# Spare matmuls at TensorE's waits, and new issue slots for every block, in an attention-plus-snake kernel

## The chip, the cores and the metric

The kernel runs on one core of one Trainium2 chip. The metric is the device time of one execution in microseconds (us), as a median over runs; less is better. A profile is one more execution, recorded on the chip. Its span is about 1.8 us shorter than the time that is reported for the same execution, so spans are compared with spans and times with times. Each run also carries a mean granted TensorE clock (1.00 is full speed). A run is called slow if it is over 1.5% above the fastest of the same kernel; ratios use the other runs, called fast.

## The reference, cut to what matters

```python
# x (8, 8, 512, 64), state (8, 8, 32, 64)
scores = scale * x @ state^T ;  a  = softmax(scores)  ; xread = a @ state
scores2 = scale * state @ x^T ; a2 = softmax(scores2) ; sread = a2 @ x
y = concat(xread, sread)                    # (8 * 544, 512), heads side by side
h = y @ w_in                                # 512 -> 2048
g = h + sin(alpha * h)**2 / (alpha + 1e-9)  # "snake"
out = g @ w_out                             # 2048 -> 512
```

## The kernel before: the parts that matter

One block is one batch. In a block, sixteen slots f each compute one 128x512 tile h_ps (the attention weights AT times M, where M is state times w_in, made in four steps), its sine on ACT, the square of the sine on POOL or VectorE, and then "snake" on VectorE, which writes gT and frees the buffer of h_ps. There are four such buffers. The second product with w_out (`mm2`, tile o_ps) lags by a block and fills the gaps of TensorE. A ninth block does the rows of sread.

```python
psH = ...tile_pool(name="psH", bufs=4, PSUM)      # h_ps
psO = ...tile_pool(name="psO", bufs=2, PSUM)      # o_ps, and the spare matmuls
def warm_up(n):                                   # spare matmuls: zeros, nobody reads them
    if n: wp = psO.tile([P, S], FP32, ...)
    for _ in range(n): nc.tensor.matmul(wp[:], warm[:, 0:P], warm[:], ...)
def pack(a, g):                                   # L240: x of a batch, reordered, on VectorE
    nc.vector.tensor_copy(a.xp[...], xnat_l[a.b][...])
def mm1(t, f):
    ... matmuls h_ps ...
    nc.scalar.activation(s, hp, ACT.Sin, scale=alpha_sb[:, f])
    if f in SQ[kind(t)]: late.append((s2, s, n))  # square later, on VectorE (L410)
    else: nc.gpsimd.tensor_tensor(s2, s, s, mult) # square now, on POOL (L403)
def snake(...): nc.vector.scalar_tensor_tensor(gT, s2, inva, hp, mult, add)   # L413
...
for b in range(B):                                # which slot issues what; BATCH is a table
    p = BATCH[min(b, 3)]; s0 = (b - 1) * 16
    if b > 1: add(post, s0 + p["L"], load_x, b, 1)            # x of batch b, POOL writes descriptors
    if b: pack at s0 + p["P"]; scores at p["S"]; exp at p["X"]; row sums at p["R"]
          normalise at p["N"] (on POOL, or on VectorE for g in ND); AT at p["A"]
    m_step(b, k, p["MA"][k]) at b * 16 + p["M"][k]            # MA: copy on ACT (1) or VectorE (0)
for t in range(B + 1):
    for f in range(16):
        cur = mm1(t, f); <pe of this slot>; snake of two slots ago
        squares left from the slot before; <mm2 of this slot>; <post of this slot>
```

(Shortened; the whole kernel follows.)

The softmax here doesn't subtract the row's maximum and nothing guards it: scores larger than these inputs give would overflow.

Of the kernel before, what the change touches and what calls it, by code (L numbers as in the profile page):

```python
# [19 lines left out]



BATCH = {0: {'M': (-13, 0, 6, 7), 'MA': ((1, 0), (1, 1), (1, 0), (1, 1))},
 1: {'P': (1, 1),
     'T': (3, 3),
     'S': (3, 3),
     'X': (3, 3),
     'R': (4, 6),
     'N': (7, 10),
     'A': 13,  # L30
     'M': (-5, -2, 3, 9),
     'MA': ((1, 1), (1, 1), (1, 1), (0, 1)),
     'W': (5, 5)},
 2: {'L': -9,
     'P': (-1, -1),
     'T': 1,
     'S': (6, 6),
     'X': (6, 6),
     'R': (7, 9),
     'N': (7, 11),  # L40
     'A': 14,
     'M': (-5, -2, 6, 10),
     'MA': ((1, 1), (0, 0), (1, 1), (0, 1)),
     'W': (-1, -1)},
 3: {'L': -19,
     'P': (-12, -9),
     'T': -9,
     'S': (2, 2),
     'X': (2, 2),
     'R': (4, 5),  # L50
     'N': (4, 11),
     'A': 11,
     'M': (-3, 1, 4, 8),
     'MA': ((1, 1), (1, 1), (1, 1), (1, 1)),
     'W': (-1, -1)}}

SQ = {0: (0, 4, 8, 9, 12, 15),
 1: (3, 5, 6, 7, 11),
 2: (2, 5, 7, 8, 9, 12, 15),
 7: (0, 5, 6, 11, 13, 15),  # L60
 8: (0, 1, 2, 3, 6, 9, 13, 15)}
ND = {1: (), 2: (), 3: (0, 1)}
XS0 = 0

TWO0 = (0, 0, 0, 1, 3, 0, 3, 0, 0, 1, 2, 3, 2, 2, 2, 2)
TWO1 = (2, 5, 3, 1, 1, 3, 3, 0, 3, 4, 9, 3, 0, 1, 4, 1)
TWO = (3, 7, 3, 9, 2, 4, 9, 4, 2, 3, 1, 6, 3, 3, 2, 3)
WARM = (9, 2, 1, 1)
LATER = 6

LOADS = ('i0', 'i1', 'x1', 'o0', 'i2', 'i3', 'o1', 'o2', 'o3')
# [3 lines left out]
def kernel(  # L75
# [11 lines left out]
    B, H, S, D = x.shape  # L87
    Ns = state.shape[2]
    P = nc.NUM_PARTITIONS
# [97 lines left out]
    def warm_up(n):  # L187
        if n:
            wp = psO.tile([P, S], FP32, name="o_ps", tag="o")
        for _ in range(n):  # L190
            nc.tensor.matmul(wp[:], warm[:, 0:P], warm[:], start=True, stop=True)

    def kind(t):
        return t if t < 2 or t >= B - 1 else 2


    def prep_state():
        st2 = const.tile([P, 16, 2, D], BF16, name="st2")
        for half, copy in ((0, nc.vector.tensor_copy), (1, nc.scalar.copy)):
            js = slice(half * 8, (half + 1) * 8)  # L200
            copy(st2[:, js], st_nat[:, js].unsqueeze(2).to_broadcast([P, 8, 2, D]))
        for half in range(2):
            tp = psH.tile([P, 8, P], BF16, name="st_ps", tag="h")
            for k in range(8):
                nc.tensor.transpose(
                    tp[:, k, :],
                    st2[:, half * 8 + k].rearrange("p r d -> p (r d)"),
                    ident[:],
                )
            for r in range(2):  # L210
                rows = slice(r * D, (r + 1) * D)
                src = tp[rows].rearrange("d k (e r2 jh) -> d e r2 jh k", r2=2, jh=2)
                dst = stT[rows].rearrange(
                    "d bg (h2 r2 jh hf k) -> d (bg h2) r2 jh hf k", h2=2, r2=2, jh=2, hf=2
                )
                nc.scalar.copy(dst[:, :, r, :, half, :], src[:, :, r])

    def prep_alpha():
        tp = psH.tile([P, FT], FP32, name="al_ps", tag="h")
        nc.tensor.transpose(tp[:], alpha_rows[:], ident_f[:])  # L220
        nc.scalar.copy(alpha_sb[:], tp[:])
# [132 lines left out]
    def m_step(b, fs, on_act):  # L354
        if fs == 0:
            Ms[b] = mpool.tile([P, G, DFF], BF16, name="M")
        if b == 0 and fs == 0:
            mp = [psH.tile([P, FW], FP32, name="m0_ps", tag="h") for _ in range(G)]
        else:
            mp = [psX.tile([P, FW], FP32, name="m_ps", tag="px") for _ in range(G)]  # L360
        for h in range(2):
            for g in range(G):
                for r in range(2):
                    rows = slice(r * D, (r + 1) * D)
                    c0 = h * 2 * Ns + r * Ns
                    o0 = h * 2 * Ns + (r ^ g) * Ns
                    nc.tensor.matmul(  # L367
                        mp[g][o0:o0 + Ns, :],
                        stT[rows, b * G + g, c0:c0 + Ns],
                        w_in_sb[rows, 2 * g + h, fs * FW:(fs + 1) * FW],  # L370
                        start=True, stop=True,
                    )
        for g in range(G):
            dst = Ms[b][:, g, fs * FW:(fs + 1) * FW]
            if on_act[g]:
                nc.scalar.copy(dst, mp[g][:])  # L376
            else:
                nc.vector.tensor_copy(dst, mp[g][:])


    def mm1(t, f):
# [17 lines left out]
        s2 = sinp.tile([P, S], BF16, name="s2")  # L399
        if f in SQ[kind(t)]:  # L400
            late.append((s2, s, n))
# [58 lines left out]

    warm_up(WARM[0])
    prep_state()
    prep_alpha()
    warm_up(WARM[1])
    a = atts[0] = Att(0)
# [4 lines left out]
    a.T(1)  # L470
    warm_up(WARM[2])
    a.S(0)
# [6 lines left out]
        load(*w)  # L479
    a.Rs(1)  # L480
    a.N(1, nc.vector)
    m_step(0, 0, (True, True))
    a.W(psO, "o")
    a.Cs()
    warm_up(WARM[3])
    nc.scalar.activation(tiny[:, 1:2], warm[:, 0:1], ACT.Sin)
    a.AT_([0])
    a.AT_([1])
# [5 lines left out]
    pe, post, two = {}, {}, {}  # L494

    def add(d, s, fn, *args):
        d.setdefault(s, []).append((fn, args))
# [8 lines left out]
    for b in range(B):  # L506
        p = BATCH[min(b, 3)]
        s0 = (b - 1) * FT
        if b > 1:
            add(post, s0 + p["L"], load_x, b, 1)  # L510
        if b:
            add(post, s0 + p["P"][0], first, b)
            for g in range(G):
                add(post, s0 + p["P"][g], att, b, "pack", g)
            if b == 1:
                for g in range(G):
                    add(pe, s0 + p["T"][g], att, b, "T", g)
            else:
                add(post, s0 + p["T"], att, b, "T_dma")
            for g in range(G):  # L520
                add(pe, s0 + p["S"][g], att, b, "S", g)
                add(post, s0 + p["X"][g], att, b, "X", g)
                add(post, s0 + p["R"][g], att, b, "Rs", g)
                eng = nc.vector if g in ND[min(b, 3)] else nc.gpsimd
                add(post, s0 + p["N"][g], att, b, "N", g, eng)
            if b == 1:
                add(pe, s0 + p["A"], att, b, "AT_", [0, 1])
            else:
                add(post, s0 + p["A"], att, b, "AT_dma")
        s0 = b * FT  # L530
        if b:
            add(pe, s0 + p["W"][0], att, b, "W")
            add(pe, s0 + p["W"][1], att, b, "Cs")
        add(post, s0 + (p["W"][1] if b else XS0), att, b, "xs")
        for k in range(0 if b else 1, FS):
            add(pe, s0 + p["M"][k], m_step, b, k, p["MA"][k])

    def rows(t, counts, todo):
        for f, c in enumerate(counts):
            two[t * FT + f] = [args for args in todo[:c]]  # L540
            del todo[:c]

    todo = [(0, st, ft, ft + 1) for ft in range(FT) for st in (0, 1)]
    rows(0, TWO0, todo)
    todo += [(0, st, ft, ft + 1) for st in (2, 3) for ft in range(FT)]
    rows(1, TWO1, todo)
    assert not todo
    for t in range(2, B + 1):
        todo = [(t - 1, st, ft, ft + 1) for st in range(C) for ft in range(FT)]
        rows(t, TWO if t < B - 1 else (4,) * FT, todo)  # L550

# [53 lines left out]
```

## Time and profile before

| | before |
|---|---|
| median of 3 runs | 231.87 us (231.43 to 232.74) |
| span of the profile | 231.4 us |
| TensorE, VectorE, ACT, POOL busy | 94%, 75%, 73%, 46% |
| start of sin of f = 9, block 0 | 30.29 |
| start of sin of f = 12, block 0 | 33.34 |
| start of blocks 1, 2 and 8 (first sin) | 37.80, 58.99, 200.05 |

The last rows are milestones, read from ACT's records: the same instruction in two kernels shows how far one is ahead.

```profile
29.68 1.05 POOL L298 TENSOR_TENSOR A<-E,rR 128x512 bf16<-128x512 bf16 x1
30.67 0.95 POOL L143 DMA_DIRECT2D xnat<-in_x_dram  x1
31.73 1.03 POOL L403 TENSOR_TENSOR s<-s 128x512 bf16<-128x512 bf16 x1
```

Both squares took 0.75 us together, and there is a gap of 0.1 us between POOL's descriptors and its next square.

### The profile page before, as it was taken

The numbers are of one execution on the slowest core, as the hardware profiler recorded it, in microseconds if no ns is written. First come the engines' busy times: TensorE is split into PE (matmuls) and PEld (weight loads), VectorE is DVE, ScalarE is ACT, GpSimd is POOL, SyncE is SP. The second block draws the span as 40 slices with busy tenths as digits, with TensorE's granted clock in tenths as the row PEclk, the third lists the DMA queues.
The fourth block names the chain that finished last, engine by engine and source line by source line (L and its number), as shares of the span: only waits on it lengthen the run. The fifth ranks groups of instructions, "written<-read, shape, count | busy, mean of one in ns | idle before, by whom it ended". The sixth has DMA issues, their size and how long they took to land.

```text
span 231.4 us, 4164 instructions
## 1 busy us (share of the span) xinstructions
PE 216.4 (94%) x1508; PEld 103.7 (45%) x1534; DVE 174.4 (75%) x306; ACT 169.8 (73%) x277; POOL 106.4 (46%) x112
## 2 busy tenths in 40 slices
PE   7776989899999999999999999999999999999992
PEld 2534243444544444445444444444444444556562
DVE  3779589989969995998699878988698665744310
ACT  4696797898697769886988788878887876544420
POOL 3864398439732652366145705451543635123300
PEclk9996799999999999999999999999999999999999
DMA  6999998855915390449036702610212111111112
GB/s 218 189 202 206 206 125 112 203 74 111 132 52 136 91 139 18 133 123 139 1 113 162 113 23 93 165 62 4 87 49 78 57 49 47 48 45 47 48 47 92
DMA packets 36662, 23.36 MB, mean 101 GB/s; under 512 B 19728, under 2 KB 32288, under 8 KB 36640
## 3 DMA queue, kind: packets, MB, share of 16 engines
q0 software_dynamic: 11504, 7.87, 24.4%
q1 hardware_dynamic: 24864, 14.95, 21.8%
q10 hardware_dynamic: 272, 0.27, 0.4%
q8 instruction: 12, 0.20, 0.4%
q14 instruction: 10, 0.08, 0.1%
HBM read 17.31 MB, written 8.91 MB: 113 GB/s over the span
## 4 chain that ended last, share of the span: by engine, by line
PE 84%; DMA 6%; DVE 6%; issue 1%; POOL 1%
PE o_ps L422 48%; PE h_ps L386 22%; DMA xnat<-in_x_dram 4%; PE m_ps L367 4%; PE h_ps L392 3%; DVE gT L413 2%; PE s_ps L277 2%; DMA st_nat<-in_state_dram 2%; PE o_ps L447 2%; PE w_ps L322 1%; DVE xp L240 1%; PE w_ps L333 1%; POOL w_in_sb L166 1%; DVE s L410 0%; DVE rC L342 0%
## 5 line engine op out<-in xcount | busy, mean ns | idle before, releaser
L422 PE MATMUL o_ps<-w_out_sb,gT 128*128 128x512 bf16 x506 | 133.5, 381 | 2.5 <-issue 1.7
L403 POOL TENSOR_TENSOR s<-s 128x512 bf16<-128x512 bf16 (+1 forms) x84 | 87.2, 1045 | 104.6 <-ACT s L398 102.4
L398 ACT ACTIVATE s<-h_ps,alpha_sb 128x512 bf16<-128x512 f32 (+1 forms) x144 | 94.7, 672 | 37.4 <-PE h_ps L386 24.6
L413 DVE SCALAR_TENSOR_TENSOR gT<-s,inva_sb,h_ps 128x512 bf16<-128x512 bf16 (+1 forms) x144 | 99.6, 710 | 25.0 <-POOL s L403 23.3
L386 PE MATMUL h_ps<-AT,M 128*128 128x512 bf16 x252 | 76.0, 385 | 1.5 <-DVE gT L413 1.0
L422 PEld LDWEIGHTS <-gT 128*128 128x128 bf16 x528 | 48.7, 98 | 57.5 <-issue 7.6
L386 PEld LDWEIGHTS <-M 128*128 128x128 bf16 x256 | 25.2, 99 | 31.6 <-issue 3.5
L376 ACT CAST M<-m_ps 128x512 bf16<-128x512 f32 x59 | 31.7, 594 | 0.6 <-PE m_ps L367 0.6
L410 DVE TENSOR_TENSOR s<-s 128x512 bf16<-128x512 bf16 (+1 forms) x60 | 27.4, 463 | 5.7 <-ACT s L398 5.2
L428 ACT COPY o_sb<-o_ps 128x512 f32<-128x512 f32 x33 | 19.6, 593 | 9.7 <-PE o_ps L422 9.0
L367 PE MATMUL m_ps<-w_in_sb,stT 64*32 64x512 bf16 x256 | 13.3, 393 | 0.9 <-DMA w_in_sb<-in_moe_w_in_dram 0.7
L290 DVE TENSOR_REDUCE R<-E 128x16 f32<-128x512 bf16 x16 | 10.9, 679 | 3.8 <-ACT E L286 3.8
L286 ACT ACTIVATE E<-s_ps 128x512 bf16<-128x512 f32 x16 | 8.9, 595 | 3.2 <-PE s_ps L277 3.0
L367 PEld LDWEIGHTS <-stT 64*32 64x32 bf16 x256 | 3.7, 89 | 14.6 <-issue 13.9
L392 PE MATMUL h_ps<-xs_all,w_in_sb 128*128 128x256 bf16 x64 | 9.6, 273 | 0.0
L342 DVE RECIPROCAL rC<-w_ps 128x128 f32<-128x128 f32 x8 | 7.6, 948 | 2.3 <-PE w_ps L333 2.2
L286 ACT ACT_TABLE_LOAD x7 | 9.0, 1283 | 0.1
L398 ACT ACT_TABLE_LOAD x7 | 9.0, 1283 | 0.1
L392 PEld LDWEIGHTS <-w_in_sb 128*128 128x128 bf16 x64 | 6.3, 98 | 4.1
L240 DVE COPY xp<-xnat 128x1024 bf16<-128x1024 bf16 x14 | 7.4, 536 | 1.0 <-DMA xnat<-in_x_dram 1.0
L277 PE MATMUL s_ps<-stT,xT 128*128 128x64 bf16 x128 | 6.0, 199 | 1.3 <-DVE xT L255 1.0
L277 PEld LDWEIGHTS <-xT 128*128 128x128 bf16 x128 | 5.2, 101 | 3.4 <-DVE xT L255 1.4
(52 smaller groups left out, 96.1 us busy)
## 6 DMA issues: line engine op xcount, KB each, us to landing
out_dram<-o_sb SPq DMA_DIRECT2D x32, 256.0 KB, 2.3
xnat<-in_x_dram POOLq DMA_DIRECT2D x7, 512.0 KB, 6.0
w_in_sb<-in_moe_w_in_dram POOLq DMA_DIRECT2D x4, 512.0 KB, 10.3
w_out_sb<-in_moe_w_out_dram POOLq DMA_DIRECT2D x4, 512.0 KB, 15.5
x_first<-in_x_dram SPq DMA_DIRECT2D x2, 512.0 KB, 5.3
st_nat<-in_state_dram SPq DMA_DIRECT2D x1, 512.0 KB, 3.7
out_dram<-o_sb SPq DMA_DIRECT2D x1, 128.0 KB, 2.4
out_dram<-o_sb ACTq DMA_DIRECT2D x1, 128.0 KB, 2.7
```

The costliest lines, as they stand in the source:

```text
L277: nc.tensor.matmul(sp[:, i, cols], a.xT[:, i, 2 * g + k, :], stT[:, a.b * G + g, cols], start=True, stop=True,)
L286: nc.scalar.activation(a.E[:, g], a.sp[g][:], ACT.Exp, scale=scale)
L367: nc.tensor.matmul(mp[g][o0:o0 + Ns, :], stT[rows, b * G + g, c0:c0 + Ns], w_in_sb[rows, 2 * g + h, fs * FW:(fs + 1) * FW], start=True, st ...
L376: nc.scalar.copy(dst, mp[g][:])
L386: nc.tensor.matmul(hp[:, :n], Ms[t][:, g, f * P:(f + 1) * P], atts[t].AT[:, g, :], start=(g == 0), stop=(g == G - 1),)
L392: nc.tensor.matmul(hp[:, :n], w_in_sb[:, q, f * P:(f + 1) * P], xs_all[:, q].rearrange("p h k b l -> p (h k b l)"), start=(q == 0), stop=( ...
L398: nc.scalar.activation(s[:, :n], hp[:, :n], ACT.Sin, scale=alpha_sb[:, f:f + 1])
L403: nc.gpsimd.tensor_tensor(s2[:, :n], s[:, :n], s[:, :n], ALU.mult)
L410: nc.vector.tensor_tensor(s2[:, :n], s[:, :n], s[:, :n], ALU.mult)
L413: nc.vector.scalar_tensor_tensor(gT[t][:, f, :n], s2[:, :n], inva_sb[:, f:f + 1], hp[:, :n], ALU.mult, ALU.add)
L422: nc.tensor.matmul(op[:], gT[t][:, ft, st * P:(st + 1) * P], w_out_sb[:, ft, :], start=(ft == 0), stop=(ft == FT - 1),)
L428: nc.scalar.copy(o_sb[:], op[:])
```

## The change

The intent: give TensorE spare work where it waits for w_in, for batch 1's x and for batch 1's scores, so that its clock stays up, and re-tune the slots of all blocks to the new pace. The core of the diff (shortened; the new counts of `mm2` per slot, in `TWO0`, `TWO1` and `TWO`, and the lists `SQ` of blocks 1 and later are cut):

```diff
-BATCH = {0: {'M': (-13, 0, 6, 7), 'MA': ((1, 0), (1, 1), (1, 0), (1, 1))},
+BATCH = {0: {'M': (-6, 1, 6, 9), 'MA': ((0, 1), (1, 1), (1, 0), (1, 1))},
  1: ...  -'R': (4, 6), 'N': (7, 10),
          +'R': (4, 7), 'N': (6, 9),
  2: ...  -'L': -9,  'T': 1,  'R': (7, 9),  'N': (7, 11), 'A': 14, 'M': (-5, -2, 6, 10),
          +'L': -7,  'T': -1, 'R': (7, 10), 'N': (7, 10), 'A': 11, 'M': (-5, -2, 5, 10),
  3: ...  -'P': (-12, -9),  'T': -9,  'R': (4, 5), 'N': (4, 11), 'A': 11, 'M': (-3, 1, 4, 8),
          +'P': (-13, -11), 'T': -10, 'R': (3, 3), 'N': (4, 9),  'A': 13, 'M': (-3, 1, 5, 8),
          -'MA': ((1,1),(1,1),(1,1),(1,1))
          +'MA': ((1,1),(0,1),(1,0),(1,0))
-SQ = {0: (0, 4, 8, 9, 12, 15),
+SQ = {0: (0, 1, 4, 8, 9, 12, 15),
-ND = {1: (), 2: (), 3: (0, 1)}
+ND = {1: (), 2: (), 3: ()}
-WARM = (9, 2, 1, 1)
+WARM = (10, 3, 0, 5, 0, 5, 4)
...
+    warm_up(WARM[3])           # ahead of M's first step, which waits for w_in
     m_step(0, 0, (True, True))
...
-    warm_up(WARM[3])           # behind the column sums
+    warm_up(WARM[4])
...
+                add(pe, s0 + p["T"][0], warm_up, WARM[5])   # ahead of batch 1's transposes
...
+                add(pe, s0 + p["S"][0], warm_up, WARM[6])   # ahead of batch 1's scores
```

More of the change, by code (lines that the diff above doesn't have):

```diff
@@ L27 @@
      'X': (3, 3),
-     'R': (4, 6),
-     'N': (7, 10),
+     'R': (4, 7),
+     'N': (6, 9),
      'A': 13,
@@ L33 @@
      'W': (5, 5)},
- 2: {'L': -9,
+ 2: {'L': -7,
      'P': (-1, -1),
-     'T': 1,
+     'T': -1,
      'S': (6, 6),
      'X': (6, 6),
-     'R': (7, 9),
-     'N': (7, 11),
-     'A': 14,
-     'M': (-5, -2, 6, 10),
+     'R': (7, 10),
+     'N': (7, 10),
+     'A': 11,
+     'M': (-5, -2, 5, 10),
      'MA': ((1, 1), (0, 0), (1, 1), (0, 1)),
@@ L45 @@
  3: {'L': -19,
-     'P': (-12, -9),
-     'T': -9,
+     'P': (-13, -11),
+     'T': -10,
      'S': (2, 2),
      'X': (2, 2),
-     'R': (4, 5),
-     'N': (4, 11),
-     'A': 11,
-     'M': (-3, 1, 4, 8),
-     'MA': ((1, 1), (1, 1), (1, 1), (1, 1)),
-     'W': (-1, -1)}}
-SQ = {0: (0, 4, 8, 9, 12, 15),
- 1: (3, 5, 6, 7, 11),
- 2: (2, 5, 7, 8, 9, 12, 15),
- 7: (0, 5, 6, 11, 13, 15),
- 8: (0, 1, 2, 3, 6, 9, 13, 15)}
-ND = {1: (), 2: (), 3: (0, 1)}
+     'R': (3, 3),
+     'N': (4, 9),
+     'A': 13,
+     'M': (-3, 1, 5, 8),
+     'MA': ((1, 1), (0, 1), (1, 0), (1, 0)),
+     'W': (-1, -1)}}
+SQ = {0: (0, 1, 4, 8, 9, 12, 15),
+ 1: (5, 6, 7, 11),
+ 2: (1, 2, 3, 5, 6, 9, 10, 11),
+ 7: (0, 2, 3, 7, 9, 11),
+ 8: (0, 5, 7, 8, 9, 10, 13, 14)}
+ND = {1: (), 2: (), 3: ()}
 XS0 = 0
-TWO0 = (0, 0, 0, 1, 3, 0, 3, 0, 0, 1, 2, 3, 2, 2, 2, 2)
-TWO1 = (2, 5, 3, 1, 1, 3, 3, 0, 3, 4, 9, 3, 0, 1, 4, 1)
-TWO = (3, 7, 3, 9, 2, 4, 9, 4, 2, 3, 1, 6, 3, 3, 2, 3)
-WARM = (9, 2, 1, 1)
+TWO0 = (0, 0, 0, 0, 2, 2, 3, 0, 0, 3, 3, 3, 1, 1, 1, 1)
+TWO1 = (1, 6, 4, 2, 0, 4, 2, 1, 3, 4, 8, 5, 0, 1, 1, 2)
+TWO = (5, 6, 2, 8, 5, 5, 6, 3, 5, 4, 0, 6, 7, 0, 2, 0)
+WARM = (10, 3, 0, 5, 0, 5, 4)
 LATER = 6
```

## The prediction

> **What bounds the kernel now.** I read the page's busy table and its row of slices first, then the busy times by stretch, then TensorE's waits and the timeline of the one stretch that stands out. All times are microseconds from the start of the span.
>
> ```profile
> PE 216.4 (94%) x1508; PEld 103.7 (45%) x1534; DVE 174.4 (75%) x306; ACT 169.8 (73%) x277; POOL 106.4 (46%) x112
> ...
> PE   7776989899999999999999999999999999999992
> ...
> PEclk9996799999999999999999999999999999999999
> ```
>
> Each digit is a slice of 5.8 us. From the sixth slice on TensorE is full at the full clock; only the first five have gaps, and the fourth and fifth (17.4 to 28.9) also have a low granted clock. So I asked for the busy times of those stretches and of the later blocks:
>
> ```profile
> core 0: us, PE busy (x) PEld busy (x) DVE busy (x) ACT busy (x) POOL busy (x), PEclk, DMA share, GB/s
> 15.96:18.07 2.11, 0.06 (x2) 0.01 (x1) 1.15 (x3) 2.09 (x5) 1.38 (x2) 1.00 1.25 206
> 18.07:19.25 1.18, 0.62 (x9) 0.45 (x9) 1.15 (x2) 1.00 (x1) 1.18 (x2) 1.00 1.24 205
> 19.25:20.63 1.38, 0.68 (x9) 0.45 (x9) 1.38 (x3) 0.00 (x0) 0.83 (x1) 0.65 1.24 207
> 20.63:26.48 5.85, 5.85 (x34) 2.33 (x34) 3.70 (x7) 4.13 (x6) 0.37 (x1) 0.50 1.24 206
> 26.48:30.00 3.52, 2.50 (x24) 0.96 (x18) 3.21 (x6) 2.96 (x6) 2.98 (x4) 1.00 1.24 207
> ...
> 80.00:100.00 20.00, 19.63 (x143) 9.18 (x145) 17.36 (x32) 17.01 (x28) 8.21 (x8) 1.00 0.45 93
> 100.00:120.00 20.00, 19.79 (x150) 9.02 (x150) 16.36 (x28) 16.08 (x27) 10.21 (x10) 1.00 0.42 92
> ```
>
> The columns are busy time (and instructions) by engine, then the clock. While batch 1's x is awaited TensorE does 0.06 of 2.11 us; in the next 2.56 us it has only 1.30 us of small transposes; then the clock falls at about 19.66 and stays at half until 26.48. The later blocks are TensorE-bound: 19.6 to 19.8 of 20. A block repeats every 23.9 us in the timeline, and its work alone, at the spacing seen there (96 matmuls of 512 columns at 0.216, four steps for M at about 0.44, scores, W and column sums about 1.6), is 20.7 + 1.8 + 1.6 = 24.1. There is no slack to win in these blocks.
>
> TensorE's waits between 12 and 34, and what the vector and POOL engines did then:
>
> ```profile
> PE x_ps L252 <- DVE xp L240: 2.6, 2, 2.1
> PE h_ps L386 <- DVE gT L413: 0.9, 1, 0.9
> PE s_ps L277 <- DVE xT L255: 0.7, 1, 0.7
> ```
>
> ```profile
> 16.70 3.39 POOL L403 TENSOR_TENSOR s<-s 128x512 bf16<-128x512 bf16 x3 [2.07 <-ACT s L398]
> ...
> 17.07 2.12 DVE L240 COPY xp<-xnat 128x1024 bf16<-128x1024 bf16 x2 [0.96 <-DMA xnat<-in_x_dram]
> 19.22 0.75 DVE L413 SCALAR_TENSOR_TENSOR gT<-s,inva_sb,h_ps 128x512 bf16<-128x512 bf16 x1
> ```
>
> x of batch 1 lands at 17.05. The two packing copies then take 0.94 and 1.26, though the copies of the whole trace have a median of 0.42, because three POOL squares run beside them. Transposes, xT, scores and exp follow in a chain. VectorE is 7.9 of 8.0 busy from 36 to 44, so there it is nearly a second bound.
>
> [...]
>
> **The change part by part.** The order of instructions of both kernels was compared on each engine; the loads of weights and of x1 keep their order.
>
> 1. Spare matmuls at the start. The first group grows from 9 to 10 (0.43 apart there), the second from 2 to 3 and the third falls from 1 to 0 (0.216 apart). State's transposes start some 0.28 later, but the vector copies that the scores wait for hide it. A group of five, 5 x 0.216 = 1.08, goes in front of the first step for M, where TensorE now waits 0.74 for w_in: that step slips by about 0.35; the single one behind the column sums (0.22) goes. The first h_ps comes perhaps 0.2 later. x1 still lands at 17.05, so this costs nothing at the end: cost about 0.
>
> 2. Five spare matmuls before batch 1's transposes and four before its scores: 1.08 and 0.86 us. The first fill half of the 2.11 us wait[...]; the second fill the 0.7 us before the scores and may overshoot by 0.2.[...] I expect the clock to stay at full. In 20.63 to 26.48 TensorE was busy all of 5.85 us at half: at full rate that work needs about 2.9, so **2.9 us** is the most that this gives.
>
> 3. The square of f = 1 moves from POOL to VectorE, before x1 lands. M's second step moves from slot 0 to slot 1, so sin of f = 2 ends at about 17.7. POOL is then free at 17.07, and both copies should take about 0.42: they end at about 17.9, not 19.2, **1.3 us** earlier. ACT's exp table now loads from about 18.4 to 19.7 (1.28), so exp starts at 19.7 to 20.0 rather than 21.27, and sin of f = 4 at about 22.4 rather than 23.78: 1.35 of it arrives.
>
> 4. Together: sin of f = 4 at 22.4, its square 0.42, snake 0.7, so h_ps of f = 8 gets its buffer at about 24.2; it starts at 28.15 now. That is 3.9 of local gain, less than the plain sum of 4.2. But POOL squares f = 5, 6 and 7 at 1.05 each, so f = 11 comes at about 27.7 against 31.12: 3.4. And slot 9 now asks for the second quarter of w_out. The loads run at 206 GB/s until about 30.5; at about 2.55 us for a half-megabyte load, the first quarter lands at 19.4 (7.87 + 11.5 us to landing), the second between 26 and 27.3. So f = 9's slot ends at about 27.0 to 27.4, where it ended at 30.26: **2.9 to 3.3**.
>
> 5. The later slots. Three of eight M copies of a block go from ACT to VectorE (3 x 0.59 off ACT, 3 x about 0.69 on), N goes from VectorE to POOL (2 x 0.88 off), one more square goes to VectorE (+0.46). VectorE rises by 2.07 + 0.46 - 1.76 = 0.8 us a block, ACT falls by 1.8. All stay below 23.9 us: VectorE about 21.4, from the counts by their means. TensorE's work is unchanged, so I give it 0, with 0.5 either way.
>
> Fourteen more spare matmuls add 14 x 0.216 = 3.0 us of TensorE work, nearly all in waits. Sum: -3.1, 0.1 given back, -3.0 net: 231.87 - 3.0 = **228.9**.
>
> **The rivals.** (a) The clock falls anyway, in all or some executions[...]: then only part 3 is left, some 1 us, and 230.5 to 231. For it: five matmuls with a gap behind them may be too few. Against: the earlier gaps, such as the 0.74 before the first M step, lowered no clock. (b) VectorE becomes the bound of blocks 0 and 1: it is over 90% busy from 27.4 to 60, so a faster TensorE would wait for snake. Its own work shifts forward too (its wait of 1.8 us on m_ps at 24.9 goes), so I expect most to pass; else the gain stops at 2.0 and the time is near 229.9. (c) A wait for the second or third quarter of w_out takes the place of the one removed; already in the sum at 3.0, and if the loads land later than I place them, another 0.5 to 1 is lost. (d) The new slots of the steady blocks save: 0.3 us in each of six would make 227. Against it stands TensorE at 98 to 99%. If the added VectorE load makes TensorE wait instead, 0.3 in each of six gives 230.7.
>
> **Range and chances.** The centre is 228.9. (a), (b) or (d) in its bad form put it at 230 to 231; (d) in its good form with the full 3.9 puts it at 226.5 to 227.5. Eight in ten: 227.2 to 230.9. Two per cent is 4.64 us, so faster needs less than 227.2; that takes the whole local gain and more besides: 0.12. Slower by 2% would need a wait in every block: 0.02.
>
> **What will show it.** The clock stays at 1.00 between 16 and 30 (part 2). The two copies of x1 take near 0.4 each and the second transpose group starts before 19 (part 3). The h_ps of f = 9 starts at about 26 and the last wait on the way is a w_out transfer or POOL (part 4). Later blocks still repeat every 23.9 us with TensorE at 98% or more (part 5). A half clock between 19 and 27, or a period other than 23.9 by over 0.2, would make the prediction wrong.

What the trace of the kernel before shows is where the clock fell (19.66), and that it was at half for 6.82 us.

## More of the kernel before

In block 0, VectorE's two squares of f = 8 and 9 ran while POOL wrote descriptors (the orders for a transfer) for batch 2's x. This is the timeline of VectorE and of POOL from 29.6 to 32 (start, duration, instruction, count):

```profile
30.79 0.75 DVE L410 TENSOR_TENSOR s<-s 128x512 bf16<-128x512 bf16 x2
```

## The result, and the profile after

| | before | after |
|---|---|---|
| median | 231.95 us (4 runs) | 235.99 us (4 runs, 235.25 to 236.07) |
| ratio of fast runs | 1 | 1.0164 (95%: 1.0128 to 1.0200) |
| span of the profile | 231.4 | 233.5 |
| start of sin of f = 9, block 0 | 30.29 | 27.13 (-3.16) |
| start of sin of f = 12, block 0 | 33.34 | 34.62 (+1.28) |
| start of blocks 1, 2 and 8 | 37.80, 58.99, 200.05 | 39.88, 61.37, 202.43 |

A ratio is the mean time of one kernel's fast runs over that of the other's fast runs of the same rounds, so it is not quite the ratio of the medians in the table. The changed kernel is 1.6% slower, not 1.3% faster.

The page of the changed kernel, busy times and the two rows of slices:

```profile
PE 221.7 (95%) x1548; PEld 104.4 (45%) x1548; DVE 177.3 (76%) x316; ACT 161.6 (69%) x262; POOL 108.8 (47%) x117
...
PE   7898859999999999999999999999999999999993
...
PEclk9999988999999999999999999999999999999999
```

The fourth slice of TensorE has risen from 6 to 8, and the clock of the fourth and fifth from 6 and 7 to 9: in this execution the waits for batch 1's x are filled and the clock stays up. The sixth slice of TensorE (29 to 35) has fallen from 8 to 5, and the clock dips to 8 just there and in the next one. The busy times by stretch, first of the kernel before and then of the changed one (busy time and instructions of each engine, then the clock):

```profile
27.00:31.00 4.00, 3.14 (x21) 1.22 (x20) 3.96 (x8) 3.31 (x7) 3.46 (x5) 1.00 1.20 200
31.00:34.00 3.00, 3.00 (x23) 1.17 (x22) 2.54 (x5) 2.82 (x5) 2.90 (x4) 1.00 0.59 59
34.00:37.00 3.00, 2.85 (x26) 1.40 (x26) 2.38 (x5) 2.23 (x5) 2.83 (x4) 1.00 0.91 125
```

```profile
27.00:31.00 4.00, 3.76 (x30) 1.39 (x30) 3.18 (x5) 3.11 (x6) 3.98 (x5) 1.00 1.24 209
31.00:34.00 3.00, 0.55 (x3) 0.15 (x2) 3.00 (x3) 0.78 (x2) 1.57 (x2) 0.83 1.08 135
34.00:37.00 3.00, 3.00 (x16) 1.55 (x14) 1.17 (x3) 1.37 (x2) 0.33 (x1) 0.60 0.40 54
80.00:100.00 20.00, 20.00 (x152) 9.00 (x151) 18.12 (x33) 15.59 (x25) 10.23 (x10) 1.00 0.44 87
```

From 31 to 34 TensorE does 0.55 of 3 us. VectorE is busy for all 3 us, and yet with only three instructions. The later blocks are full on TensorE, as before, and their period in the milestones is 23.89 in both kernels. TensorE's waits from 12 to 40, and the timeline of VectorE and POOL in the changed kernel:

```profile
PE h_ps L386 <- DVE gT L413: 3.9, 5, 2.4
```

```profile
28.64 0.75 DVE L413 SCALAR_TENSOR_TENSOR gT<-s,inva_sb,h_ps 128x512 bf16<-128x512 bf16 x1 [0.80 <-POOL s L403]
29.31 3.56 DVE L410 TENSOR_TENSOR s<-s 128x512 bf16<-128x512 bf16 x2
32.79 2.05 DVE L413 SCALAR_TENSOR_TENSOR gT<-s,inva_sb,h_ps 128x512 bf16<-128x512 bf16 x3
```

```profile
26.56 1.05 POOL L298 TENSOR_TENSOR A<-E,rR 128x512 bf16<-128x512 bf16 x1
27.57 1.04 POOL L403 TENSOR_TENSOR s<-s 128x512 bf16<-128x512 bf16 x1
28.56 1.05 POOL L301 TENSOR_TENSOR A<-E,rR 128x512 bf16<-128x512 bf16 x1
29.55 0.95 POOL L143 DMA_DIRECT2D xnat<-in_x_dram  x1
30.52 2.05 POOL L403 TENSOR_TENSOR s<-s 128x512 bf16<-128x512 bf16 x2
```

The two squares that took 0.75 us take 3.56. The trace's single records give 0.59 to the first and 3.05 to the second, which started at 29.82 and ended at 32.87, 0.30 us after POOL's last square (30.52 + 2.05 = 32.57). Meanwhile no snake could free an h_ps buffer; TensorE waited 2.45 us for one, and the clock fell to half from 32.99 to 36.41. The lead of 3.16 us at f = 9 had become a delay of 1.28 at f = 12 and of 2.08 at the start of block 1.

### The profile page after: what moved, and what is told of

Read it like the earlier page. It is cut to its first block, busy times and chain, and to the rows that moved or that the text cites. A ratio compares the mean times of both kernels' runs of the same rounds, so it can differ in the third digit from the quotient of the medians.

```text
span 233.5 us, 4226 instructions
## 1 busy us (share of the span) xinstructions
PE 221.7 (95%) x1548; PEld 104.4 (45%) x1548; DVE 177.3 (76%) x316; ACT 161.6 (69%) x262; POOL 108.8 (47%) x117
## 4 chain that ended last, share of the span: by engine, by line
PE 80%; DMA 6%; DVE 5%; POOL 5%; ACT 1%; issue 1%; POOLq 0%; ACTq 0%
PE o_ps L422 47%; PE h_ps L386 21%; DMA xnat<-in_x_dram 4%; PE m_ps L367 4%; POOL s L403 3%; PE h_ps L392 3%; DMA st_nat<-in_state_dram 2%; PE o_ps L447 2%; DVE s L410 1%; PE s_ps L277 1%; PE w_ps L322 1%; DVE gT L413 1%; PE w_ps L333 1%; ACT s L398 1%; POOL w_in_sb L166 1%
## 5 line engine op out<-in xcount | busy, mean ns | idle before, releaser
L403 POOL TENSOR_TENSOR s<-s 128x512 bf16<-128x512 bf16 (+1 forms) x79 | 78.8, 1007 | 105.4 <-ACT s L398 97.1
L422 PEld LDWEIGHTS <-gT 128*128 128x128 bf16 x528 | 49.3, 98 | 57.6 <-issue 5.7
L386 PEld LDWEIGHTS <-M 128*128 128x128 bf16 x256 | 24.1, 98 | 34.2 <-issue 7.5
L410 DVE TENSOR_TENSOR s<-s 128x512 bf16<-128x512 bf16 (+1 forms) x65 | 30.5, 482 | 8.3 <-ACT s L398 7.8
L376 ACT CAST M<-m_ps 128x512 bf16<-128x512 f32 x44 | 24.5, 591 | 0.8 <-PE m_ps L367 0.8
L378 DVE CAST M<-m_ps 128x512 bf16<-128x512 f32 x20 | 13.7, 688 | 6.2 <-PE m_ps L367 6.0
L298 POOL TENSOR_TENSOR A<-E,rR 128x512 bf16<-128x512 bf16 x8 | 9.1, 1138 | 5.2 <-DVE rR L291 5.2
L191 PE MATMUL o_ps<-warm 128*128 128x512 bf16 x27 | 8.8, 473 | 1.3 <-DVE warm L177 1.3
```

Source lines behind the costliest of these rows:

```text
L376: nc.scalar.copy(dst, mp[g][:])
L378: nc.vector.tensor_copy(dst, mp[g][:])
L386: nc.tensor.matmul(hp[:, :n], Ms[t][:, g, f * P:(f + 1) * P], atts[t].AT[:, g, :], start=(g == 0), stop=(g == G - 1),)
L403: nc.gpsimd.tensor_tensor(s2[:, :n], s[:, :n], s[:, :n], ALU.mult)
L410: nc.vector.tensor_tensor(s2[:, :n], s[:, :n], s[:, :n], ALU.mult)
L422: nc.tensor.matmul(op[:], gT[t][:, ft, st * P:(st + 1) * P], w_out_sb[:, ft, :], start=(ft == 0), stop=(ft == FT - 1),)
```

## The experiments

The first theory was S: this one stalled square takes the gain. The rivals were that it was an accident of one execution, and that VectorE and POOL simply had too much to do in block 0. All kernels computed the right result. Most edits are single table entries.

**The changed kernel again** (no edit).

> The changed kernel once more, unedited, for a second profile. Theory S (one stalled square): VectorE's square of f = 9 in block 0 takes about 3 us again (3.05 in the first profile, 0.42 elsewhere), and sin of f = 12 starts about 1.3 us later than in the kernel before, though sin of f = 9 starts 3 us earlier. Rival R (the stall was an accident of one execution, and the loss is spread over later blocks): no long square, and the loss of 4 us shows elsewhere. Both: about 236.

Median 236.36 (231.82 to 236.89), against 232.60 for the kernel before. Three of the four executions are called slow, because the fourth ran in 231.82; they lie close to the first four runs of the same kernel (235.25 to 236.07). The profile, one of the three, has a second square of 3.05 us again, at 31.89. So the stall was no accident of one execution, though an execution without the loss exists. The lead at f = 9 was not 3 us but 1.09 in this profile: the clock was at half from 19.61 to 23.02 in spite of the spare matmuls.

**The square of f = 9 given to POOL.**

```diff
-SQ = {0: (0, 1, 4, 8, 9, 12, 15),
+SQ = {0: (0, 1, 4, 8, 12, 15),
```

> The changed kernel with the square of f = 9 of block 0 given to POOL; nothing else. Theory S: without the stalled square sin of f = 12 comes some 2 to 3 us earlier and the time falls to about 232.5 to 233.5 (POOL pays 1.05 for the square more). Rival V (VectorE and POOL together have too much to do in block 0, whichever of them squares): the time stays within 0.5 us of the changed kernel, 235.5 to 236.5.

Median 233.63, ratio to the kernel before 1.0078 (0.9995 to 1.0161), where the changed kernel had 1.0164. No square is over 1.3 us:

```profile
31.33 0.58 DVE L410 TENSOR_TENSOR s<-s 128x512 bf16<-128x512 bf16 x1
```

POOL has more to do than in the changed kernel, and still the time is less: this speaks against the rival of too much work, and about half of the loss seems to hang on this square (the two intervals still touch).

**Batch 2's x loaded at slot 7, so that descriptors no longer stand behind the second normalisation.**

```diff
- 2: {'L': -7,
+ 2: {'L': -9,
```

> The changed kernel with batch 2's x loaded at slot 7 as in the kernel before (its descriptors are written on POOL ahead of the second normalisation, not behind it). Theory S in its form with descriptors[...]: no square over 1.3 us, about 232.5 to 233.5. If the descriptors play no part: a square of about 3 us remains, about 236.

Runs of 231.97 and 232.16, and 235.91 and 236.91 (called slow). The profile, one of the latter, has a square of 3.55 us, now that of f = 8. The stall moved rather than went.

**The kernel before with the spare matmuls alone** (WARM and the three `warm_up` lines of the diff above).

> The kernel before with the spare matmuls of the change alone. If the spare matmuls save the clock (the prediction's part 2): clock at 1.00 from 16 to 30, and 1.0 to 2.9 us faster than the kernel before, 229 to 231. If the executions that are timed do not have the half clock that the first profile shows: within 0.5 us of the kernel before. If spare matmuls delay the start: up to 0.5 us slower.

Ratio 0.9994 (0.9928 to 1.0061). The clock did what the change wanted: from 0.997 to 1.00 in four executions, where the kernel before had 0.981 to 0.998. In the profile (span 230.0) it is 2.8 us ahead of the kernel before at the start of block 1 (35.00 against 37.80). Then the lead shrinks to 1.4, at the packing of batch 2:

```profile
35.74 1.61 DVE L240 COPY xp<-xnat 128x1024 bf16<-128x1024 bf16 x2 [0.82 <-DMA xnat<-in_x_dram]
```

VectorE waited 0.82 us for batch 2's x to land, and its second copy then took 1.26 beside two POOL squares. A faster block 0 had run into a transfer.

**The same, run again with more rounds.**

> The kernel before with the spare matmuls alone, a second time with more rounds, to size them: 0 to 0.7% less than the kernel before (the first time 0.9994 with an interval of 0.6% either way), with less spread (231.4 to 232.0 then, against 230.2 to 235.1).

0.9992 (0.9958 to 1.0026), clock 0.992 to 1.00. Spare matmuls alone are worth nothing that these runs can see.

**The changed kernel without its spare matmuls** (WARM = (9, 2, 1, 0, 1, 0, 0)).

> The changed kernel with the spare matmuls of the kernel before. If the spare matmuls are what keeps the clock up at batch 1's x: the half clock returns between about 19 and 26.5 and the time rises by 0 to 2 us over the changed kernel, to 236 to 238 (less than the 2.9 of the prediction, since the stalled square comes after it). If they do not matter, or only delay the start: 235.5 to 236.5. The stalled square of about 3 us is expected to stay unless the later arrival of f = 8 and 9 changes what POOL does beside it.

Ratio 1.0064 (0.9982 to 1.0146): taking the spare matmuls out did not make it slower; the expectation missed. In its profile there was no stall and no half clock at batch 1's x (x1 had landed early, at 16.66), and it was 4.26 us ahead at f = 9. Of that, 2.4 was left at the start of block 1. It lost this in block 1, where the new slots pack batch 3 one slot earlier. VectorE's timeline:

```profile
42.21 1.13 DVE L240 COPY xp<-xnat 128x1024 bf16<-128x1024 bf16 x1 [2.65 <-DMA xnat<-in_x_dram]
```

It waited 2.65 us for x of batch 3, and the clock was at half from 46.01 to 49.43. The lead of 2.4 us at the start of block 1 was a delay of 1.9 at the start of block 2.

**Batch 2's x loaded at slot 11** ('L': -5).

> The changed kernel with batch 2's x loaded at slot 11: no descriptors are written beside the squares of f = 8 and 9, but POOL's second normalisation and two squares still follow each other without a gap. If the stall needs POOL to be writing descriptors when VectorE's square starts: no square over 1.3 us, some 2 to 3 us less than the changed kernel, 233 to 234, unless the later landing of x2 makes a new wait before the packing of batch 2 (about 37 to 40). If a run of back-to-back POOL instructions is enough: a square of 2 to 3 us again, about 235.5.

Ratio 1.0082 (1.0004 to 1.0160). No square over 1.3 us in the profile, but the packing of batch 2 waited 1.65 us for its x, and a lead of 4.2 us at f = 9 ended as a delay of 0.2. The later landing took what the stall had taken. The run can't tell the two theories apart: POOL stood idle for 0.94 us while these squares ended, so the unbroken row was not there either.

**Batch 1's row sums and normalisation in the slots of before.**

```diff
-     'R': (4, 7), 'N': (6, 9),
+     'R': (4, 6), 'N': (7, 10),
```

> The changed kernel with batch 1's row sums and normalisation in the slots of the kernel before (R 4, 6 and N 7, 10): the second normalisation on POOL comes behind the square of f = 10 and the descriptors are written behind the first normalisation. If it is this order on POOL[...]: no square over 1.3 us, 232.5 to 234. If the stall only moves to another square: about 235.5.

Ratio 1.0042 (0.9966 to 1.0119), just clear of the changed kernel's 1.0128 to 1.0200 (other rounds), and no square over 1.3 us. That fits a stall that depends on the order of work on POOL. One profile doesn't show it: the run without the spare matmuls had no stall in the changed order either.

**That, and the packing and transposes of batches 3 and later in the slots of before** ('P': (-12, -9), 'T': -9).

> The changed kernel with batch 1's row sums and normalisation and the later batches' packing and transposes in the slots of the kernel before (R 4, 6; N 7, 10; P -12, -9; T -9). It takes away both suspects: the stalled square, and the packing of batch 3 one slot earlier, ahead of the landing of its x[...]. If these two are the whole loss: no square over 1.3 us, no wait of VectorE for x over 0.3 us, and the time is that of the kernel before or up to 1.5 us less, 230.5 to 232.5. If other slots lose too: 233 to 234.

Ratio 0.9971 (0.9904 to 1.0037; one of six runs, 235.49, is called slow and left out). With both suspects out, the changed kernel is level with the kernel before. It still has all the rest of the change: the other slots, the copies moved to VectorE and the spare matmuls. As far as these runs resolve it, the two suspects are the whole loss. Their shares are less sure: 1.0164 to 1.0042 for the normalisation and 1.0042 to 0.9971 for the packing come from different sets of rounds, and the second step lies inside the intervals. In the changed kernel's own profile the packing of batch 3 waited only 0.39 us, and the delay grew only from 2.08 us at the start of block 1 to 2.38 at that of block 2; so there nearly all of the loss lies before block 1.

**What makes the square stall.** In the first stall POOL was writing descriptors (29.55 to 30.50) when the square started (29.82). Theory Q was a guess from that: a square that starts there is long if a POOL product that waits for nothing stands behind the descriptors. So I put such a product into the kernel before:

```diff
             nc.gpsimd.dma_start(xnat[...], xv[...])
+        if b == 2: nc.gpsimd.tensor_tensor(spare[:], warm[:], warm[:], ALU.mult)
```

> The kernel before with one more POOL instruction, a 128x512 product of zeros that waits for nothing, right behind the descriptors of batch 2's x. [...] Then the square of f = 8, which took 0.42 us in the kernel before though it started 0.1 us after the descriptors did, takes about 2 us (to the end of the added product and 0.3 more), and the time rises by 0.5 to 1.5 us. Rival: the stalls of the changed kernel had another reason; the squares then take 0.4 to 1.3 us.

Ratio 1.0238 (1.0176 to 1.0300). The kernel before now has the fault, larger than expected and on the square of f = 9 where f = 8 was expected. VectorE's squares (of 0.42 and 4.90; line numbers are 3 higher in this run):

```profile
29.49 5.24 DVE L413 TENSOR_TENSOR s<-s 128x512 bf16<-128x512 bf16 x2
```

It ended at 34.73, 0.29 us after the fourth POOL product in a row. The control, with the product ahead of the descriptors:

> Control for the run with the product behind the descriptors: the same product ahead of them, so that POOL has the same work but nothing ready behind the descriptors. Theory Q: the squares of f = 8 and 9 take 0.4 to at most 1.3 us (one POOL instruction), none takes 2. Rival (it is POOL's amount of work that stalls the squares): as in the other run.

Two executions at 232.67 and 233.37 (fast; ratio 1.0031, 0.9954 to 1.0108) and two at 237.72 and 238.57 (called slow). The profile, of a slow one, has a square of 4.04 us. As a control it failed: POOL was delayed, so its next square had become ready behind the descriptors after all.

The cleaner test keeps the added product at slot 7 and moves the descriptors away to slot 5:

> The kernel before with the added POOL product that waits for nothing at slot 7, where the descriptors of batch 2's x stood, and those at slot 5: POOL has the same work, back to back, but writes no descriptors when the squares of f = 8 and 9 start. Theory Q[...]: the squares take 0.4 to 1.3 us, none takes 2, and the time is at most 1.5 us over the kernel before. Rival (any run of back-to-back POOL instructions does it): a square of 2 to 5 us, and 236 to 238 as with the product behind the descriptors.

Ratio 1.0265 (1.0223 to 1.0307). That the stall needs descriptors is wrong, and the rival holds. VectorE and POOL of this run:

```profile
30.86 4.91 DVE L410 TENSOR_TENSOR s<-s 128x512 bf16<-128x512 bf16 x2
```

```profile
30.12 1.05 POOL L298 TENSOR_TENSOR A<-E,rR 128x512 bf16<-128x512 bf16 x1
31.12 1.03 POOL L499 TENSOR_TENSOR spare<-warm 128x512 bf16<-128x512 bf16 x1
32.12 1.03 POOL L403 TENSOR_TENSOR s<-s 128x512 bf16<-128x512 bf16 x1
33.12 1.04 POOL L301 TENSOR_TENSOR A<-E,rR 128x512 bf16<-128x512 bf16 x1
34.12 1.03 POOL L403 TENSOR_TENSOR s<-s 128x512 bf16<-128x512 bf16 x1
```

The first of the two squares started at 30.86 and took 4.57, to 35.43: it ended 0.28 us after the fifth of five POOL products in an unbroken row (34.12 + 1.03 = 35.15). The second then took 0.41. No descriptors were being written. Beside the squares of 3.05, 4.90 and 4.57 us (changed kernel, product behind the descriptors, this run) POOL ran without a gap of over 0.02 us, until 0.30, 0.29 and 0.28 us before the square's end. That descriptors play no part where they do stand in the row is not shown: in the changed kernel the square was not done from 29.89 to 30.51 while POOL wrote descriptors and did nothing else.

What stays open is which squares are long. One pair bears on it. In the run without the spare matmuls the second square began 0.27 us behind the start of the descriptors, just as in the changed kernel, and took 0.41. There the sine that POOL's next square needs ended at 29.20, when VectorE was done (29.13); in the changed kernel it ended at 29.37, before VectorE's square began (29.82). The pair fits a guess that the square is long when POOL's next product is ready before it starts. The guess is not shown, and other squares speak against it: with the added product ready behind the descriptors, the first square still took 0.42, and in the run with f = 9 on POOL the square took 0.58 (31.33 to 31.91), though the next POOL product followed at once.

**Looking for a version that beats both.** The spare matmuls and batch 2's x at slot 5, on the kernel before ('L': -11):

> The kernel before with the spare matmuls, and batch 2's x loaded at slot 5 instead of 7. In the run with the spare matmuls alone (its span 230.0) the packing of batch 2 waited 0.8 us for x2[...], and a gain of 2.8 us shrank to 1.4. If the late landing of x2 is what took it: x2 lands about 1 us earlier, the wait goes, and the profile's span falls to about 228.7 to 229.5, timed 230 to 231. If w_out's loads or VectorE limit there anyway: 231 to 232 as in the run with the spare matmuls alone.

Ratio 1.0002 (0.9943 to 1.0062). The wait for x2 is gone, but in the profile x1 landed at 17.59, behind the start of POOL's squares, and its two packing copies took 1.25 and 1.26 each. With the square of f = 1 on VectorE and M's second step at slot 1 as well:

> The kernel before with the spare matmuls, x of batch 2 loaded at slot 5, the square of f = 1 on VectorE and M's second step at slot 1. If the earlier free POOL lets the packing of batch 1 run[...] (0.4 us a copy instead of 1.25) in most executions and no new wait for x2 follows: profile span 228 to 229.5 and 0.5 to 1% less time than the kernel before. If x1 lands so that the copies still meet POOL's squares: as in the run without the last two, no faster than the kernel before.

1.0023 (0.9973 to 1.0072); the copies took 1.21 and 1.26, as x1 landed at 17.38. One square is not enough to clear POOL. With the square of f = 2 on VectorE too, first on the changed kernel with the two suspects out, then on the kernel before with the spare matmuls:

```diff
-SQ = {0: (0, 4, 8, 9, 12, 15),
+SQ = {0: (0, 1, 2, 4, 8, 9, 12, 15),
- 2: {'L': -9,
+ 2: {'L': -11,
```

> The changed kernel with normalisation and packing in the slots of the kernel before, the square of f = 2 on VectorE too, and batch 2's x at slot 5. POOL then starts its first square about 0.7 us later (f = 3), so both packing copies of batch 1 should take 0.4 us wherever x1 lands between 16.7 and 18. If this lottery is the main spread left: runs within 1.5 us of each other and 230 to 231.5, 0.5 to 1% less than the kernel before. If not: as the run without it, 230.5 to 233.8.

> The kernel before with the spare matmuls, the squares of f = 1 and 2 on VectorE and batch 2's x at slot 5. Same reason as for the other run with the square of f = 2 on VectorE: 229.8 to 231.3, 0.5 to 1% less than the kernel before; if VectorE has too much to do in block 0: 231 to 233.

Ratios 0.9945 (0.9913 to 0.9977) and **0.9925 (0.9891 to 0.9958)**. In the first one's profile one of the two copies still took 1.17 us, since x1 landed at 17.90 and POOL's first square started at 17.77; its median of 231.75 is just above the range expected. The second has a median of 230.99 us, five of its six runs within 0.35 us, and beats both kernels. In its profile VectorE packs x1, which landed at 17.58, by the time that POOL's first square starts:

```profile
17.60 0.76 DVE L240 COPY xp<-xnat 128x1024 bf16<-128x1024 bf16 x2
```

```profile
18.34 1.03 POOL L403 TENSOR_TENSOR s<-s 128x512 bf16<-128x512 bf16 x1 [3.23 <-ACT s L398]
```

It is 2.20 us ahead of the kernel before at the start of block 1, and still 2.20 at block 8. Last, this version without the spare matmuls, and with them again, on one chip:

> The best version so far (kernel before, spare matmuls, squares of f = 1 and 2 on VectorE, batch 2's x at slot 5) without the spare matmuls. If the spare matmuls are worth time once their lead is not given back at the packing of batch 2: the half clock returns in most executions and the time is 0.5 to 1.2% above the version with them, at that of the kernel before. If the moved squares and load are the whole gain: within 0.3% of the version with them.

> The version with the spare matmuls again, on the same chip as the run without them: 0.5 to 1% less than the kernel before, as the first time (0.9925).

0.9974 (0.9929 to 1.0020) without, 0.9938 (0.9900 to 0.9977) with them. The clock is 0.983 to 0.996 without and 0.996 to 1.00 with them. So the version is confirmed, and the spare matmuls may be worth some 0.4% in it; the intervals overlap, and that stays open.

## Why the prediction was wrong

By its own parts:

- **What bounds the kernel**: right. Later blocks repeat every 23.89 us in both kernels, with TensorE full.
- **Part 1** (the start costs about nothing): right; sin of f = 0 starts at 14.47 against 14.37.
- **Part 2** (the clock stays up): right for the first profile, where it is 1.00 until 32.99. Not sure in every execution, as rival (a) had it: of the 14 profiles with the spare matmuls, four have the clock at half for 3.41 us after the wait for batch 1's x (the repeat from 19.61 to 23.02). Of the six without them, three have 3.41 us there, one has 6.83 and two have none. Its size was the maximum from one profile of the kernel before, with 6.8 us at half clock. In later executions that kernel's mean clock lies anywhere from 0.974 to 0.998, so this time differs from one execution to the next.
- **Part 3** (both copies of x1 at 0.42, 1.3 us earlier): half right. In the first profile the copies took 0.43 and 1.26, since x1 landed at 17.20 and POOL's square started at 17.37. It gained 0.56 at f = 4 where I expected 1.35. Landings between 16.46 and 18.13 in the profiles make this a lottery.
- **Part 4** (f = 9's slot ends 2.9 to 3.3 earlier): near, and in part by luck. The sine of f = 9 starts 3.16 earlier, but the slot itself, which ends where the next h_ps begins, ends at 27.96 against 30.26, 2.3 earlier. Part 3 brought 0.8 us less than was counted in, sin of f = 4 starting at 23.22 instead of 22.4; and the wait for w_out that was to hold slot 9 back did not come. At f = 11 it was already wrong: h_ps started at 29.44, not at 27.7. Part 4 had counted POOL's squares of f = 5, 6 and 7 alone, but the new slots put a normalisation of 1.05 us (26.56) ahead of that of f = 7 (27.57).
- **The step that failed** is the one behind the sum: that the lead at f = 9 goes through to the end. It stood in rival (b), "Its own work shifts forward too [...] so I expect most to pass". I had counted how busy VectorE is, and asked whether its work would fit. I had not asked what its instructions would meet. The square of f = 9 met an unbroken row on POOL and took 3.05 in place of 0.42: 2.6 us on the chain that frees h_ps buffers, and a half clock of 3.42 us behind it. Before that 1.5 us had already been given back between f = 9 and f = 11, with VectorE's wait of 0.80 for POOL's square of f = 7.
- **Rival (c)** (a transfer takes the place of the wait removed) named w_out, which was not it. The transfers that bite are x of batches 2 and 3, for which VectorE's packing waited 1.65 and 2.65 us in two experiments. Part 5 gave the new slots of later blocks 0, with 0.5 either way; the packing one slot earlier was in them.
- **Rival (d)** in its bad form did not occur. The extra load of VectorE that part 5 counted, 0.8 us a block, did not appear either: in block 4 VectorE is busy 20.2 us before and 20.0 after (ACT 19.9 and 18.3, near the 1.8 less that was expected).

The profile of the changed kernel against that of the kernel before shows a loss of 2.0 us, and the timed runs 1.64%, or 3.8. The first profile of the kernel before was one of its longer executions: its fast spans in later rounds run from 228.4 to 232.0.

## What to carry to other kernels

A lead in one stage is worth something only if what follows can take it. Before you count on it, lay the instructions of the engines beside each other at the new times: which of them will run beside each other (the square beside POOL's row took 3.05 us in place of 0.42), and which wait for a transfer that does not move (1.65 and 2.65 us here). With spare matmuls in TensorE's waits its clock stayed up behind batch 1's x in ten of 14 profiles, without them in two of six; alone they gave no time that the runs can see; moving two squares away from the moment when x lands, and loading the next x earlier, gave 0.6 to 0.75% together with them. And look at several executions before you size a term from one profile.

## What these runs leave open

- How long a square takes beside POOL. In the changed kernel one took 0.59 us (from 29.31) beside the end of a POOL product (28.56 to 29.61), and the next 3.05 us; with five POOL products in a row one took 4.57. What decides which is long is not settled here.
- What descriptors do to a square. The runs are divided: in the kernel before two squares of 0.42 us ran inside the writing of descriptors (30.67 to 31.62), but in the changed kernel a square was not done in 0.62 us (29.89 to 30.51) in which POOL wrote descriptors and did no product; the sine that its next product needs had ended at 29.37.
- What lowers the clock. In the kernel before it fell at 19.66, when the longest gap of TensorE had been 2.05 us, with only small transposes in the 1.6 us behind it; TensorE was busy for 1.03 of the 3.41 us before the fall. In the changed kernel it fell at 32.99, inside a wait of 2.45 us; of the 3.41 us before (29.58 to 32.99) TensorE was busy for 1.55. It came back after 6.82 and 3.42 us. Two falls show no rule.
- Whether matmuls of zeros keep it up. With the spare matmuls as the only edit its mean was 0.992 to 1.00 in ten executions, against 0.974 to 0.998 for the kernel before. It did not stay up in every execution with them (part 2 above).
